# Chunked attention and a squared-ReLU feed-forward layer: one values step moved into an output stage, one transpose moved to the end of an input stage, and four steps moved by half a slot

## The chip, the cores and the metric

The kernel runs on one core of one Trainium2 chip. The metric is the device time of one execution in microseconds (us), as the median of several runs. The profile comes from one further execution of the same program. Its span, from the first to the last instruction, is a little shorter than the device time of that execution.

The engines are named as in the profile: PE is the matrix engine, PEld its weight loads (they overlap PE), DVE the vector engine, ACT the scalar engine, POOL the GpSimd engine, and SP the engine whose queue issues the loads and the transposes by DMA. Every engine works its instructions off in the order in which the program gives them.

## The reference, cut to what matters

```python
# q, k, v: [8, 8, 576, 64]; attention inside chunks of 64 tokens
scores = q_c @ k_c.T / 8
attn = exp(scores - max); attn = attn / (sum + 1e-9)
out = attn @ v_c
x = out.transpose(0, 2, 1, 3).reshape(4608, 512)
h = maximum(x @ w_in, 0)          # w_in  [512, 2048]
y = (h * h) @ w_out               # w_out [2048, 512]
```

Inputs and output are float32; the matrix products are done in bf16 with float32 sums.

## The kernel before, in words

The 4608 tokens are 18 groups of 256, numbered 0 to 17, and two groups make a block, 0 to 8. A block passes through three kinds of work.

*Attention of a group.* The loads of q, k and v are issued on SP. q and k are cast to bf16 (`C`) and transposed by DMA (`TD`). `scores` (`SC`, L474 and the exponential on ACT, L485) makes 32 small matmuls and one ACT instruction. `values` (`AV`, or its halves `AV0` and `AV1` for the group's first and second 128 tokens) makes 16 small matmuls of L501 a half into a bank of PSUM. DVE then takes the reciprocal of the sums (L435) and multiplies (L436), which gives x. `transpose_x` (`XT`) makes eight transposes on PE (L531) into a bank of PSUM and one copy on ACT (L536), which gives a half of xT. For blocks 6 and 8 it is a DMA instead.

*Input stage* of blocks 0 to 3: for each of 16 slices of 128 hidden units (`ft` 0 to 15), four matmuls of 512 columns (L570), a ReLU on ACT (L581), and the square on DVE (L588) or ACT (L586). The result is gT. For blocks 4 to 8 the stage goes in 16 "quads" of seven products (`A1`, `B2`, `A6`, `C5`, `A7`, `C3`, `A4`, L647, four matmuls of 256 columns each), a form of fast matrix multiplication with seven products in place of eight. DVE adds two partial results and takes the ReLU (L655), ACT copies partial results out (L683, L689, L692), and the square falls to ACT (L664), DVE or POOL (L666).

*Output stage*: block 0 goes plainly (L883). From block 1 on there are seven products of 16 matmuls each (L766) in the same fast form, over sums of gT that DVE makes (`g_sum`, L604: `d4`, `d5`, `d3`, `d2`). The first two products of block 2 are `p2`, which needs no sum, and `p1`, which needs `d4`. `d4` is made in two halves, the first at slot 14 of the input stage, the second at slot 15. After `p1` ACT copies its bank out (`keep`, L823), and the third product may add to that bank only when the copy has been made.

The order of everything is written out by hand. Blocks 0 to 3 have a plan by *slot*: one slot per `ft` (0 to 15), then one per half product of the output stage. For block 2, slots 16 to 18 are empty; 19 and 20 are `p2`, 21 and 22 are `p1`, and 23 to 32 the other five. After the work of a slot come one load and then what the plan has there, in the order in which it was entered: the sums, then `C`, `TD`, `SC`, `AV`, `XT`. From block 4 on there are four slots a quad step, and a block takes 16 slots. In slot s come first the products of the quads, then what the plan has at s − 0.5, then the half product of the block before (if the slot has one), then what the plan has at s. So 9.5 is the place in slot 10 ahead of that slot's output half, and 10 the place behind it.

While block 2 goes through its stages, the attention is that of block 3 (groups 6 and 7). While block 4 does, it is that of block 5 (groups 10 and 11); during block 6 it is that of block 7 (groups 14 and 15, whose chunks lie in different batch rows).

The PSUM banks of the attention: through block 3, `att_bank` gives `ps_att` and `ps_att2` by turns. From block 4 on there is one tile only, `ps_att`, so each user waits until the one before it has been read out:

```python
def att_bank():
    if "out" in banks:
        return ps_att.tile([128, 1024], FP32, name="ps_att")
    state["att"] = state.get("att", 0) + 1
    if state["att"] % 2:
        return ps_att.tile([128, 1024], FP32, name="ps_att")
    return ps_att2.tile([128, 1024], FP32, name="ps_att2")
```

Of the kernel before, what the change touches and what calls it, by code (L numbers as in the profile page):

```python
# [144 lines left out]
def kernel(  # L145
# [31 lines left out]
    def is_whole(g):  # L177
        return chunks[g][0][0] == chunks[g][3][0]
# [5 lines left out]
    QUADS = 4  # L184
# [130 lines left out]
    def go(pieces):  # L315
        for f in pieces:
            f()
# [288 lines left out]
    def summed(out, in0, in1, op=ALU.add):  # L606
        return lambda *_: add(out, in0, in1, op)
# [28 lines left out]
    def tock():  # L636
        state["clock"] += 1
        for x in [x for x in later if x[0] <= state["clock"]]:
            later.remove(x)
            x[1]()  # L640
# [268 lines left out]
    def pieces(grps):  # L909
        for g in grps:  # L910
            yield from qk_pieces(g)
        for g in grps:
            yield from v_pieces(g)

    SC, AV, XT = scores, values, transpose_x
    TD = transpose_qk_dma
# [67 lines left out]
    for j in range(QUADS):  # L984
        grps, nxt, far = blocks[j], blocks[j + 1], blocks[j + 2]
        plan = {}

        def at(slot, f, *x):
            plan.setdefault(slot, []).append((f, x))

        if j == 0:
            loads, go_slots = pieces(far), range(17)
            at(28, summed(b11_p_b21, b11, b21))
            for slot, f in ((24, TA), (27, SC), (29, AV), (31, XT)):
                at(slot, f, nxt[0])
            at(31, TQ, nxt[1])
            at(31, summed(b22_m_b21, b22, b21, ALU.subtract))
            phases = [first_ffn_in, ffn_out_by_ft(0)]
        elif j == 1:
            loads, go_slots = itertools.chain(*map(qk_pieces, far)), range(26, 48)  # L1000
            for slot, f in ((1, TK), (4, SC), (7, AV), (12, XT)):
                at(slot, f, grps[1])
            for i, g in enumerate(nxt):
                for slot, f in ((16 + 4 * i, C), (21 + 4 * i, TD), (36 + i, SC), (38 + 2 * i, AV),
                                (41 + 2 * i, XT)):
                    at(slot, f, g)
            for i, g in enumerate(far):
                at(36 + 4 * i, C, g)
                at(42 + 3 * i, TD, g)
            at(2, summed(b12_p_b21, b12, b21))  # L1010
            at(12, summed(b11_m_b12, b11, b12, ALU.subtract))
            at(20, summed(b12_p_b22, b12, b22))
            out_j = ffn_out(1)
            for i in (20, 27, 29, 31):
                at(i, lambda: next(out_j)())
            phases = [ffn_in(1, [(0, 256, FT_ORDER), (256, 256, FT_ORDER)]), out_j]
        else:
            out_j = ffn_out(j)
            for i in (14, 15):
                at(i, lambda: next(out_j)())  # L1020
            phases = [ffn_in(j, [(0, BT, range(n_ft))])]
            if j == 2:
                loads, go_slots = itertools.chain(*map(v_pieces, nxt), pieces(far)), [
                    *range(16), *range(27, 36)]
                slots = {SC: (6, 9), AV: (11, 14), XT: (22, 28), C: (21, 26), TD: (25, 29)}
                for f in (C, TD):
                    for i, g in enumerate(far):
                        at(slots[f][i], f, g)
                phases.append(out_j)
            else:  # L1030
                loads, go_slots = pieces(far), range(11)
                for f, slots in ((C, (11, 13)), (TD, (13, 15))):
                    for i, g in enumerate(far):
                        at(slots[i], f, g)
                slots = {SC: (2, 4), AV: (7, 10), XT: (13, 15)}
            for f in (SC, AV, XT):
                for i, g in enumerate(nxt):
                    at(slots[f][i], f, g)
            if j == 2:
                for i, f in enumerate((summed(a21_p_a22, a21, a22),  # L1040
                                       summed(a12_m_a21, a12, a21, ALU.subtract),
                                       summed(a11_p_a21, a11, a21))):
                    at(1 + 2 * i, f)
        slot = 0
        for phase in phases:
            for _ in phase:
                if slot in go_slots:
                    for f in loads:
                        f()
                        break  # L1050
                for f, x in plan.get(slot, []):
                    f(*x)
                slot += 1
        assert all(x < slot for x in plan), (j, slot, sorted(plan))
        if j < QUADS - 1:
            go(loads)
# [19 lines left out]
    for j in range(QUADS, n_blk):  # L1076
        if j == QUADS:
            n = 14 - LEAD
            slots = [1 + 19 * i // n for i in range(n)]
            assert len(slots) == n  # L1080
        else:
            slots = [s for s in range(4, 20) if s % 16 not in NO_OUT]
            start = 3
        if j == QUADS:
            between = {}
            for n in (0, 1, 2, 3):
                between.setdefault(n, []).append((load, (1, loads)))
            for n in (2, 2, 2, 3):
                between.setdefault(n, []).append((x_sums, (QUADS, len([1 for z in between.values() for y in z if y[0] is x_sums]))))
            for f, x in between.get(0, []):  # L1090
                f(*x)
            for i in range(LEAD):
                next(out_j)
                tock()
                for f, x in between.get(i + 1, []):
                    f(*x)
        else:
            outs[j - 1] = ffn_out(j - 1)
            at(j, start, lambda j=j: next(outs[j - 1])())
        for s in slots:  # L1100
            plan.setdefault(("out", 16 * (j - QUADS) + s), []).append(outs[j - 1])

        if j + 1 < n_blk:
            S0, V0, V1, X0 = ((1.5, 3.5), (4.5, 7.5), (6, 9.5), (8, 11.5)) if j == QUADS else (
                (0.5, 7), (2, 8), (3.5, 9.5), (3.5, 10)) if is_whole(blocks[j + 1][0]) else (
                (3.5, 9.5), (5, 10.5), (7, 12), (8.5, 13.5))
            for i, g in enumerate(blocks[j + 1]):
                at(j, S0[i], SC, g)
                at(j, V0[i], AV0, g)
                at(j, V1[i], AV1, g)  # L1110
                at(j, X0[i], XT, g)
            if j + 2 == n_blk:
                at(j, 22, check_sums)
                at(j, 25.5, count_bad)
            for i, s in enumerate((13.5, 15, 17.5, 18)):
                at(j, s, x_sums, j + 1, i)
        if j == QUADS:
            for s in range(4):
                at(j, 4 * s + 2, w_sums_in_place, s)
            assert next(loads, None) is None  # L1120
        if j + 2 < n_blk:
            more = pieces(blocks[j + 2])
            if j == n_blk - 3:

                for s, n in ((0, 1), (1, 1), (2, 1), (3, 1), (4, 1), (5, 1), (10, 2), (12.5, 3),
                             (14, 1), (14.5, 1), (15, 1), (15.5, 1)):
                    at(j, s, load, n, more)
            else:
                for s in range(0, 16):
                    at(j, s, load, 1 if is_whole(blocks[j + 2][0]) else 2, more)  # L1130
            for i in range(2):
                at(j, (9, 13)[i], C, blocks[j + 2][i])
                at(j, ((9.5, 13.5) if j == n_blk - 3 else (12, 13.5))[i], TD, blocks[j + 2][i])
# [66 lines left out]
```

## Time and profile before

| | us |
|---|---|
| median of 3 runs | 283.7 (282.65 to 283.81) |
| the profiled execution | 284.07, with a span of 282.3 |
| PE busy | 268.1 (95% of the span) |
| DVE busy | 201.1 (71%) |
| ACT busy | 167.9 (59%) |
| POOL busy | 91.9 (33%) |
| granted PE clock | 0.997 |

In a row of the timeline the first number is the start in us from the start of the span, the second the duration of the group in us, then the engine, the line of the code, the operation, what it writes and reads, the shape, and how many instructions the row holds. In brackets stands how long the engine was idle before it, and on whom it waited. Durations of instructions in a row overlap a little, since each begins before the end of the one before has been recorded. So the step from one start to the next is what the engine needs for it.

Block 2's input stage begins at 82.91, its output stage at 98.70; block 3's input stage begins at 112.91. Quad 0 of block 4 begins at 133.71.

### The profile page before, as it was taken

Reading aid. Unit: us, or ns where it says so; the run is one execution under the profiler, and the core shown is the slowest. Engines: PE = TensorE matmul, PEld = TensorE weight load, DVE = VectorE, ACT = ScalarE, POOL = GpSimd, SP = SyncE. Lnnn points to the kernel's source line nnn. Section 1 sums busy time; section 2 is a strip of 40 time slices with the busy share of each in tenths; the row PEclk is TensorE's granted clock in tenths of the full one; section 3 lists DMA queues with packets and bytes.
Section 4 is the critical chain, followed back from the end, with each engine's and each line's share of the span. In section 5 each row is a group of like instructions: output and inputs, shape, how many; then the busy total and the mean of one; then the engine's idle time right before and its main releaser. Section 6 shows DMA issues by size and latency. Waiting matters only on the chain.

```text
span 282.3 us, 8007 instructions
## 1 busy us (share of the span) xinstructions
PE 268.1 (95%) x3304; PEld 205.6 (73%) x3307; DVE 201.1 (71%) x367; ACT 167.9 (59%) x298; POOL 91.9 (33%) x123
## 2 busy tenths in 40 slices
PE   2989999999999989999989999999999999999994
PEld 2764444788774479447878888888788888888883
DVE  1287605899448591399989998789679877994751
ACT  1527705786448855875767775665766664756330
POOL 2047832430350002132233525442343322431612
PEclk9999999999999999999999999999999999999998
DMA  7999999999999995999999788599997340220323
GB/s 221 240 323 393 393 308 247 343 202 162 298 179 231 219 243 117 260 249 182 229 239 198 173 213 217 117 193 231 253 165 196 77 58 18 85 64 10 76 75 111
DMA packets 133368, 55.09 MB, mean 195 GB/s; under 512 B 102160, under 2 KB 129040, under 8 KB 133328
## 3 DMA queue, kind: packets, MB, share of 16 engines
q1 hardware_dynamic: 130320, 45.23, 69.7%
q0 software_dynamic: 2864, 9.18, 9.9%
q8 instruction: 27, 0.44, 0.6%
q10 hardware_dynamic: 144, 0.13, 0.1%
q14 instruction: 13, 0.11, 0.1%
HBM read 36.70 MB, written 9.44 MB: 163 GB/s over the span
## 4 chain that ended last, share of the span: by engine, by line
PE 81%; DVE 11%; ACT 3%; DMA 2%; issue 1%; SPq 0%; ACTq 0%; DVEq 0%
PE ps_ffn L647 21%; PE ps_out L766 20%; PE ps_ffn L570 15%; PE ps_ffn L766 13%; PE ps_ffn L883 5%; DVE x L436 3%; DVE gT L588 3%; PE ps_att L474 2%; PE ps_att L501 2%; DMA qk_st<-in_k_dram 2%; DVE w_st L604 2%; PE ps_att L531 1%; PE ps_ffn L426 1%; PE ps_ffn L393 1%; DVE relu L655 1%
## 5 line engine op out<-in xcount | busy, mean ns | idle before, releaser
L570 PE MATMUL ps_ffn<-xT,w_in_bf 128*128 128x512 bf16 (+1 forms) x328 | 58.7, 333 | 1.2 <-DVE xT L517 1.0
L766 PEld LDWEIGHTS <-w_st 128*128 128x128 bf16 x512 | 48.9, 98 | 8.0 <-DVE w_st L604 1.7
L655 DVE CUSTOM_DVE_ANT_0 relu<-ps_ffn,w_st 128x512 f32<-128x512 f32 x60 | 39.3, 684 | 15.2 <-PE ps_ffn L647 13.8
L581 ACT ACTIVATE relu<-ps_ffn 128x256 bf16<-128x256 f32 (+2 forms) x82 | 39.9, 503 | 12.7 <-PE ps_ffn L570 11.2
L570 PEld LDWEIGHTS <-w_in_bf 128*128 128x128 bf16 x328 | 30.9, 98 | 22.5 <-DVE xT L517 1.2
L588 DVE TENSOR_TENSOR gT<-relu 128x256 bf16<-128x256 bf16 (+2 forms) x69 | 34.3, 529 | 17.3 <-ACT relu L581 16.9
L795 POOL DMA_DIRECT2D out_dram<-o_sb x27 | 19.8, 732 | 52.1 <-DVE o_sb L604 50.1
L647 PE MATMUL ps_ffn<-qk_st,w_in_bf 128*128 128x256 bf16 x240 | 35.3, 273 | 0.0
L647 PEld LDWEIGHTS <-w_in_bf 128*128 128x128 bf16 x320 | 30.7, 98 | 4.0 <-issue 0.2
L766 PE MATMUL ps_out<-w_out_bf,w_st 128*128 128x256 bf16 x240 | 31.0, 273 | 0.4 <-DVE w_st L604 0.4
L766 PEld LDWEIGHTS <-gT 128*128 128x128 bf16 x296 | 28.5, 98 | 3.5
L689 ACT ACTIVATE w_st<-ps_ffn 128x512 f32<-128x512 f32 x20 | 11.9, 597 | 26.7 <-PE ps_ffn L647 26.7
L436 DVE TENSOR_TENSOR x<-ps_att,recs 128x512 bf16<-128x512 f32 x36 | 24.9, 691 | 1.2
L647 PEld LDWEIGHTS <-qk_st 128*128 128x128 bf16 x240 | 22.6, 98 | 2.9
L485 ACT ACTIVATE e<-ps_att 128x1024 bf16<-128x1024 f32 x18 | 18.4, 1024 | 9.5 <-PE ps_att L474 9.5
L647 PE MATMUL ps_ffn<-xT,qk_st 128*128 128x256 bf16 x160 | 23.9, 273 | 0.0
L666 POOL TENSOR_TENSOR qk_st<-relu 128x512 bf16<-128x512 f32 x10 | 10.3, 1033 | 41.6 <-DVE relu L655 38.1
L666 POOL TENSOR_TENSOR gT<-relu 128x512 bf16<-128x512 f32 x10 | 10.3, 1033 | 38.6 <-DVE relu L655 38.6
L766 PE MATMUL ps_ffn<-w_out_bf,w_st 128*128 128x256 bf16 x144 | 17.7, 273 | 0.5 <-DVE w_st L604 0.5
L664 ACT ACTIVATE gT<-relu 128x512 bf16<-128x512 f32 x28 | 17.7, 632 | 0.0
L604 DVE TENSOR_TENSOR w_st<-gT,w_st 128x1024 bf16<-128x1024 bf16 x26 | 17.5, 706 | 0.0
L445 POOL CAST qkb<-qk_st 128x1024 bf16<-128x1024 f32 x12 | 13.9, 1156 | 10.2 <-DMA qk_st<-in_k_dram 10.2
(91 smaller groups left out, 433.5 us busy)
## 6 DMA issues: line engine op xcount, KB each, us to landing
qk_st<-in_q_dram SPq DMA_DIRECT2D x16, 512.0 KB, 5.2
out_dram<-o_sb POOLq DMA_DIRECT2D x31, 256.0 KB, 4.1
qk_st<-in_k_dram SPq DMA_DIRECT2D x24, 256.0 KB, 5.4
ve_sb<-in_v_dram SPq DMA_DIRECT2D x32, 128.0 KB, 4.1
w_st<-in_moe_w_in_dram SPq DMA_DIRECT2D x8, 512.0 KB, 6.3
w_st<-in_moe_w_out_dram SPq DMA_DIRECT2D x8, 512.0 KB, 5.5
vo_sb<-in_v_dram SPq DMA_DIRECT2D x24, 128.0 KB, 3.4
qk_st<-in_k_dram SPq DMA_DIRECT2D x4, 512.0 KB, 6.0
```

What stands on the lines that cost most here:

```text
L436: nc.vector.tensor_tensor(out=x, in0=o[:, :, :, 0:D], in1=rec.to_broadcast([128, 2, n, D]), op=ALU.mult)
L485: nc.scalar.activation(out=e_out, in_=s_in, func=AF.Exp, scale=scale)
L570: nc.tensor.matmul(out=h[:, 0:n], lhsT=w_in_bf[:, dt, ft * 128:(ft + 1) * 128], rhs=xT[:, c // 128:(c + n) // 128, dt, :], start=(dt == 0) ...
L581: nc.scalar.activation(out=rl[:, 0:n], in_=h[:, 0:n], func=AF.Relu)
L588: nc.vector.tensor_tensor(out=dst, in0=src, in1=src, op=ALU.mult)
L604: nc.vector.tensor_tensor(out=out, in0=in0, in1=in1, op=op)
L647: nc.tensor.matmul(out=bank[:, f * GT:(f + 1) * GT], lhsT=a[:, dt, ft * 128:(ft + 1) * 128], rhs=b[:, :, dt, :], start=(first and f == 0 a ...
L655: nc.vector._custom_dve(TENSOR_ADD_SAT, out=out, in0=in0, in1=in1, s0=BIG, s1=0.0)
L664: engine.activation(out=dst, in_=r, func=AF.Square)
L666: engine.tensor_tensor(out=dst, in0=r, in1=r, op=ALU.mult)
L766: nc.tensor.matmul(out=out_ps, lhsT=lhsT, rhs=b[:, i, :], start=(first and i == 0 and (last or t == 0)), stop=(i == HF - 1), skip_group_ch ...
L795: dma.dma_start(out=out[t0:t0 + GT, col:col + HD].rearrange("(t p) d -> p t d", p=128), in_=o_sb.rearrange("p (t d) -> p t d", d=HD))
```

## The change

In the plan of block 2:

- `AV` of group 7 (both halves: 32 matmuls, two reciprocals, two multiplications) goes from slot 14, ahead of `ft` 15, to slot 22, behind `p1`.
- `XT` of group 6 (eight transposes, one copy on ACT) goes from slot 22 to slot 15, behind `ft` 15 and ahead of `p2`.

In the plan of block 4, for block 5's groups 10 and 11:

- `AV1` of group 11 goes from 9.5 to 10, behind the output half of slot 10.
- `XT` of group 10 goes from 8 to 8.5, behind the two products (`B2`, `C3`) of slot 9. Slot 9 has no output half.
- `XT` of group 11 goes from 11.5 to 12, behind the output half of slot 12.

In the plan of block 6, for block 7's group 15:

- `AV0` goes from 10.5 to 11, behind the output half of slot 11.

No instruction is added or removed; no tile and no load changes.

```diff
@@ j == 2 @@
-                slots = {SC: (6, 9), AV: (11, 14), XT: (22, 28), C: (21, 26), TD: (25, 29)}
+                slots = {SC: (6, 9), AV: (11, 22), XT: (15, 28), C: (21, 26), TD: (25, 29)}
@@ j >= QUADS @@
-            S0, V0, V1, X0 = ((1.5, 3.5), (4.5, 7.5), (6, 9.5), (8, 11.5)) if j == QUADS else (
+            S0, V0, V1, X0 = ((1.5, 3.5), (4.5, 7.5), (6, 10), (8.5, 12)) if j == QUADS else (
                 (0.5, 7), (2, 8), (3.5, 9.5), (3.5, 10)) if is_whole(blocks[j + 1][0]) else (
-                (3.5, 9.5), (5, 10.5), (7, 12), (8.5, 13.5))
+                (3.5, 9.5), (5, 11), (7, 12), (8.5, 13.5))
```

## The prediction

> **What bounds the kernel now.** I read the page's busy shares and the chain that ended last, then the waits of PE, then the timeline of each engine around the steps that move. PE carries the time, with 81% of the chain; by the page it is busy for 95% of the span, and its granted clock is 0.997.
>
> ```profile
> PE 81%; DVE 11%; ACT 3%; DMA 2%; issue 1%; SPq 0%; ACTq 0%; DVEq 0%
> ```
>
> So a moved step is worth what it changes in PE's gaps. The waits view names them (engine and line, on whom; us in total, times, longest). The three rows below hold the gaps that the change touches: on a sum of gT, on x, and on the exponential.
>
> ```profile
> PEld L531 <- DVE x L436: 2.1, 4, 1.0
> PEld L766 <- DVE w_st L604: 1.7, 3, 0.8
> PEld L501 <- ACT e L485: 1.1, 2, 0.7
> ```
>
> **A: block 2, values of group 7 to slot 22, first transpose to slot 15.** PE's rows now:
>
> ```profile
> 97.41 0.22 PE L501 MATMUL ps_att<-ve_sb,e 64*64 64x65 bf16 x2
> ...
> 97.82 1.04 PE L570 MATMUL ps_ffn<-xT,w_in_bf 128*128 128x512 bf16 x4
> 98.70 1.91 PE L766 MATMUL ps_ffn<-w_out_sum,gT 128*128 128x256 bf16 x16
> 100.44 0.60 PE L766 MATMUL ps_ffn<-w_out_bf,w_st 128*128 128x256 bf16 x4
> 101.58 1.48 PE L766 MATMUL ps_ffn<-w_out_bf,w_st 128*128 128x256 bf16 x12 [0.53 <-DVE w_st L604]
> 102.89 0.61 PE L531 MATMUL ps_att<-ident,x 128*128 128x128 bf16 x8
> 103.73 1.91 PE L766 MATMUL ps_ffn<-w_out_sum,w_st 128*128 128x256 bf16 x16 [0.23 <-ACT kept L823]
> ...
> 108.97 0.61 PE L531 MATMUL ps_att<-ident,x 128*128 128x128 bf16 x8
> 109.42 1.91 PE L766 MATMUL ps_ffn<-w_out_bf,gT 128*128 128x256 bf16 x16
> ```
>
> By starts, values take 0.41 (97.41 to 97.82), ft 15 0.88, p2 1.74 for 16 matmuls (0.109 each), p1 as much, eight transposes 0.45 (108.97 to 109.42). p1 stops after four matmuls, at 100.88, and goes on at 101.58: 0.70 of wait for d4's second half. DVE shows why:
>
> ```profile
> 98.69 0.20 DVE L435 RECIPROCAL recs<-ps_att 128x8 f32<-128x8 f32 x1
> ...
> 100.38 0.42 DVE L588 TENSOR_TENSOR gT<-relu 128x512 bf16<-128x512 bf16 x1
> 100.83 0.69 DVE L604 TENSOR_TENSOR w_st<-gT 128x1024 bf16<-128x1024 bf16 x1
> 101.43 2.49 DVE L604 TENSOR_TENSOR w_st<-gT,w_st 128x1024 bf16<-128x1024 bf16 x4
> ...
> 105.05 0.68 DVE L604 TENSOR_TENSOR o_sb<-ps_ffn,kept 128x512 f32<-128x512 f32 x1
> ```
>
> Group 7's two pairs of reciprocal and multiplication (98.69 to 100.38, 1.69) stand ahead of the square of ft 15, and that ahead of d4's second half. Without them the square waits only for its ReLU on ACT:
>
> ```profile
> 98.20 0.63 ACT L586 ACTIVATE gT<-relu 128x512 bf16<-128x512 bf16 x1
> 98.90 0.60 ACT L581 ACTIVATE relu<-ps_ffn 128x512 bf16<-128x512 f32 x1
> 99.39 1.04 ACT L442 CAST qkb<-qk_st 128x1024 bf16<-128x1024 f32 x1
> ...
> 103.09 0.59 ACT L823 COPY kept<-ps_ffn 128x512 f32<-128x512 f32 x1 [1.72 <-PE ps_ffn L766]
> 103.58 1.02 ACT L536 COPY xT<-ps_att 128x1024 bf16<-128x1024 bf16 x1
> ```
>
> The changed order, step by step. PE: ft 15 at 97.41 to 98.29, transposes to 98.74, p2 to 100.48, p1's first four to 100.92. ACT: the ReLU follows the square of 98.20 at 98.83, done 99.43. DVE: square 99.46, d4's second half 0.45 later (as 100.38 to 100.83), done about 100.6. That is 0.3 ahead of PE, so the 0.70 goes. p1 ends at 102.22. Then the values take their 0.41 where the transposes lay, in the shadow of ACT's copy of p1's bank. That copy comes 0.20 after the last matmul is issued (102.89 to 103.09) and frees the bank 0.64 later (103.73), so the third product starts at 102.22 + 0.84 = 103.06 against 103.73. **A gives 0.7.**
>
> What queues behind the moved pieces. On ACT, the transpose's copy (1.02) now runs ahead of group 8's casts: 99.32, 100.3, 101.3, free at 102.3, just before `keep` is due at 102.42. Even if each runs 0.1 long, PE loses 0.2. The casts end about 0.9 later, and with them TD of group 8 on SP and the three loads of v behind it; even the longest landing shown below, 7.7, has group 8's transposed q and k there by 110.1, ahead of block 3's stage (112.9). None of the moved steps issues a DMA, and none touches POOL. On DVE, group 7's 1.69 now stands behind the six remaining sums (2.49 for four, so 3.7) and the output sum (0.6): 100.6 + 3.7 + 0.6 + 1.7 = 106.6. Its transpose is due on PE at 108.97 − 0.7 = 108.3, so 1.7 to spare: no cost. The banks alternate as before, and each is read out in time (group 6's transpose copy by 100.3, the values need it at 102.2).
>
> **B: block 4, half steps.** There is one attention bank now.
>
> ```profile
> 144.92 1.05 PE L766 MATMUL ps_out<-w_out_sum,gT 128*128 128x256 bf16 x8
> 146.73 0.62 PE L531 MATMUL ps_att<-ident,x 128*128 128x128 bf16 x8 [0.77 <-DVE x L436]
> 147.19 0.60 PE L647 MATMUL ps_ffn<-xT,qk_st 128*128 128x256 bf16 x4
> ...
> 148.06 0.60 PE L647 MATMUL ps_ffn<-qk_st,qk_st 128*128 128x256 bf16 x4
> ```
> ```profile
> 145.99 0.69 DVE L436 TENSOR_TENSOR x<-ps_att,recs 128x512 bf16<-128x512 f32 x1
> 147.93 1.29 DVE L655 CUSTOM_DVE_ANT_0 relu<-ps_ffn,w_st 128x512 f32<-128x512 f32 x2 [1.25 <-PE ps_ffn L647]
> ```
>
> The output half ends at 144.92 + 0.87 = 145.79. Group 10's transpose wants the bank that group 11's first values hold until DVE has multiplied (146.68), and goes at 146.73: 0.94 idle. Moved behind B2 and C3 (147.19 to 148.06, 0.87), these fill 145.79 to 146.66; the transpose still goes at 146.73, and slot 10 follows at 147.18 in place of 148.06. **B gives 0.88**, if nothing is late next. B2 and C3 need banks, sums and weights that were all read or written by 145.8.
>
> Late next could be two steps, and the other two half steps bear on them. Group 11's second values need the bank when ACT has copied group 10's transpose, 147.35 + 1.02 = 148.4. At 9.5 they would come at 148.05 and wait 0.3; at 10 they come behind an output half, at 148.92. Group 11's transpose needs x from DVE: two ReLU sums from 146.7 to 148.0, the output sum when slot 10's half is done (149.1), a square of 0.6, then 0.83 for the pair, 151.2. At 12 it comes at 148.92 + 0.36 + 1.31 + 0.87 = 151.46 (values with their switch, three products, the half). So 0.25 to spare.
>
> **C: block 6, group 15's first values behind the output half of slot 11.**
>
> ```profile
> 200.59 0.60 PE L647 MATMUL ps_ffn<-qk_st,w_in_bf 128*128 128x256 bf16 x4
> 201.57 0.22 PE L501 MATMUL ps_att<-ve_sb,e 64*64 64x65 bf16 x2 [0.38 <-ACT e L485]
> ...
> 201.83 1.05 PE L766 MATMUL ps_out<-w_out_bf,w_st 128*128 128x256 bf16 x8
> 202.71 0.60 PE L647 MATMUL ps_ffn<-qk_st,w_in_bf 128*128 128x256 bf16 x4
> ```
>
> The product ends at 201.03 and the values wait for the exponential until 201.57. With the half first (0.87, its sum d3 written by 200.1) they go at 202.0, the exponential long done, and slot 12 follows at 202.26 against 202.71. **C gives 0.45.** Group 15's multiplication comes 0.4 later, done 203.4; the second values want the bank at 204.1.
>
> **Sum.** 0.70 + 0.88 + 0.45 = 2.03. Against the profiled execution 284.07 − 2.03 = 282.0; it was 0.37 above the median, so 283.7 − 2.03 = **281.7**. Half a per cent, 1.4 us, is about what a measurement of this kernel can tell from no change.
>
> **The rivals.** *First, POOL's casts fall on other DVE work in block 3.* DVE sets PE's wait there, and the casts are timed by loads.
>
> ```profile
> 128.95 1.51 POOL L445 CAST qkb<-qk_st 128x1024 bf16<-128x1024 f32 x1 [1.48 <-DMA qk_st<-in_k_dram]
> ```
> ```profile
> 129.48 1.52 DVE L604 TENSOR_TENSOR w_st<-gT 128x1024 bf16<-128x1024 bf16 x1
> ...
> 131.64 0.69 DVE L604 TENSOR_TENSOR w_st<-gT 128x1024 bf16<-128x1024 bf16 x1
> ```
> ```profile
> 132.39 1.48 PE L766 MATMUL ps_out<-w_out_bf,w_st 128*128 128x256 bf16 x12 [0.43 <-DVE w_st L604]
> ```
>
> The same sum takes 1.52 beside the cast and 0.69 without. If loads, casts and DVE all move 0.7 earlier, nothing changes. If the casts stay where the loads put them, one can newly fall on a square in the chain: +0.83, 282.5. Or the sum at 129.48 gets ahead of its cast: DVE gains 0.83, of which PE can use only its wait at this place, 0.4 as the row has it and 0.6 by the starts: 281.1. The Trainium skill ("SBUF — State Buffer", Who interferes with whom) says that a VectorE instruction with two SBUF inputs and a GpSimd instruction that reads SBUF share a read port, and that the later one is blocked until the first ends. By that rule, 1.52 against 0.69 agrees, and the order of issue, not my sum, would decide between 281.1 and 282.5.
>
> *Second, the wait of B comes back.* Its slack is 0.25 on DVE for group 11's x. If DVE runs behind there, PE stops at the second transpose in place of the first, and the 0.88 is lost: 282.6. Against it: DVE stood idle 1.25 ahead of 147.93, and that room is used in the new order.
>
> *Third, slower: the DMA stream does not follow.* From 112 on the loads run close behind one another on SP.
>
> ```profile
> DMA to landing us min/median/max: 4.4/5.2/7.7
> ```
> ```profile
> 129.53 4.38 SPq L451 DMA_TRANSPOSE qkT<-qkb  x2
> ```
> ```profile
> 135.98 0.44 PE L474 MATMUL ps_att<-qkT 64*64 64x64 bf16 x32
> ```
>
> Group 10's q and k are transposed by a DMA issued at 129.53; at the median landing they are there at 134.7, and their scores, after A at 135.3, have 0.6 to spare even if SP does not move. At the longest landing, 7.7, they are there at 137.2 and PE waits 1.9. Two such landings, in this block and the next, would cost 3.8: 281.7 + 3.8 = 285.5. It decides from a landing of about 5.8 on; the change is lost altogether where two land at 6.8. Against it: SP waits in block 2 for the casts of group 9 on ACT, which follow PE, so its stream moves with PE.
>
> **Chances.** Forecast 0.60 (own range 281.2 to 282.2); casts on other DVE work 0.14; B's wait back 0.11; DMA late 0.13; something else 0.02. Range: 280.9 (the 281.1 of the first rival less some spread) to 283.3 (both middle rivals together, 281.7 + 0.83 + 0.88 = 283.4, nearly), which leaves out the DMA case. Faster by over 0.5% (below 282.3): 0.64, the forecast and the good side of the first rival. Within: 0.22, the middle rivals. Slower: 0.14.
>
> **What would show it.** In A: no wait of PE on w_st between p1's fourth and fifth matmul, values between p1 and the third product, this about 5.65 after the end of ft 14 (now 6.32). In B: no gap ahead of L531 in slot 9, and quad products before it. In C: no wait on the exponential at L501. Wrong it would be by a new wait of PE on ACT's `keep` in block 2, on x at group 11's transpose, or on qkT at L474, or by a longer run of DVE in block 3.

## The result and the profile after

The changed kernel takes 281.47 us (median of 6 runs, 280.87 to 282.20) against 283.22 (6 runs, 282.65 to 283.81) of the kernel before, measured beside it: a ratio of 0.9937, with a 95% interval of 0.9916 to 0.9959. Medians are of all runs and ratios of the fast ones (slow is a run over 1.5% above its kernel's fastest), so a ratio need not be that of the two medians. The forecast was 281.7. The profiled execution took 282.2, with a span of 280.4, and the granted clock is 0.999.

First the shares of the chain that ended last, on the page after:

```profile
PE 77%; DVE 8%; DMA 6%; SPq 4%; ACT 2%; issue 1%; POOL 0%; ACTq 0%; DVEq 0%
```

PE has 77% of it, where it had 81%, and DMA with SP's queue 10%, where they had 2%; 8.3 us (2.9% of the span) of this are one landing, that of group 9's transposed q and k, to which block 3 below comes back. PE's work is the same (267.8 of busy time on the page, 268.1 before), so what was gained was gained in its gaps. The waits view has them (engine and line, on whom; us in total, times, longest):

```profile
PEld L766 <- DVE w_st L604: 1.2, 2, 1.0
...
PEld L501 <- ACT e L485: 0.4, 1, 0.4
...
PEld L531 <- DVE x L436: 0.4, 2, 0.2
```

Against the three rows of before, the transposes' wait on x fell from 2.1 to 0.4, the values' wait on the exponential from 1.1 to 0.4, and the output products' wait on w_st from 1.7 to 1.2, with a longest that rose from 0.8 to 1.0: one of those gaps is gone and another one grew.

**A in the timeline.** PE, around the end of block 2's input stage and its first output products:

```profile
97.47 0.61 PE L531 MATMUL ps_att<-ident,x 128*128 128x128 bf16 x8
97.92 1.91 PE L766 MATMUL ps_ffn<-w_out_sum,gT 128*128 128x256 bf16 x16
99.66 1.91 PE L766 MATMUL ps_ffn<-w_out_bf,w_st 128*128 128x256 bf16 x16
101.50 0.22 PE L501 MATMUL ps_att<-ve_sb,e 64*64 64x65 bf16 x2
...
102.25 1.91 PE L766 MATMUL ps_ffn<-w_out_sum,w_st 128*128 128x256 bf16 x16 [0.28 <-DVE w_st L604]
```

The transposes, p2 and p1 follow one another without a stop, all 16 matmuls of p1 stand in one row, and the third product follows p2 after 4.33 (97.92 to 102.25), where it was 5.03 (98.70 to 103.73). DVE and ACT at the same place:

```profile
98.64 0.43 DVE L588 TENSOR_TENSOR gT<-relu 128x512 bf16<-128x512 bf16 x1 [0.57 <-ACT relu L581]
99.10 0.69 DVE L604 TENSOR_TENSOR w_st<-gT 128x1024 bf16<-128x1024 bf16 x1
```
```profile
98.51 1.00 ACT L536 COPY xT<-ps_att 128x1024 bf16<-128x1024 bf16 x1
...
100.62 1.04 ACT L445 CAST qkb<-qk_st 128x1024 bf16<-128x1024 f32 x1 [0.16 <-DMA qk_st<-in_k_dram]
101.61 0.59 ACT L823 COPY kept<-ps_ffn 128x512 f32<-128x512 f32 x1
```

The square no longer stands behind group 7's multiplications, and d4's second half is done at 99.8, ahead of the fifth matmul of p1 (99.66 + 0.44). ACT gets the transposes' copy and both casts out of the way just as `keep` is due; `keep` ends at 102.20 and the third product starts at 102.25, so it is `keep`, and not the sum that the row names, that it waits for.

**B.** PE in slots 8 to 12 of block 4 and at the first product of block 5:

```profile
144.12 1.05 PE L766 MATMUL ps_out<-w_out_sum,gT 128*128 128x256 bf16 x8
145.01 0.60 PE L647 MATMUL ps_ffn<-xT,qk_st 128*128 128x256 bf16 x4
145.45 0.60 PE L647 MATMUL ps_ffn<-xT,w_in_bf 128*128 128x256 bf16 x4
145.94 0.62 PE L531 MATMUL ps_att<-ident,x 128*128 128x128 bf16 x8
146.39 0.60 PE L647 MATMUL ps_ffn<-qk_st,qk_st 128*128 128x256 bf16 x4
...
150.69 0.61 PE L531 MATMUL ps_att<-ident,x 128*128 128x128 bf16 x8
...
153.75 1.30 PE L647 MATMUL ps_ffn<-qk_st,w_in_bf 128*128 128x256 bf16 x8
154.89 0.60 PE L647 MATMUL ps_ffn<-xT,qk_st 128*128 128x256 bf16 x4
```

B2 and C3 (145.01 and 145.45) fill what was the gap, and the transposes wait for nothing. From the output half to the first product of slot 10 it was 3.14 (144.92 to 148.06) and is 2.27 (144.12 to 146.39). The last two rows hold what was not foreseen: eight matmuls (two products) take 1.14 to the next start, where they took 0.88 before. These are the rows of before:

```profile
155.42 1.04 PE L647 MATMUL ps_ffn<-qk_st,w_in_bf 128*128 128x256 bf16 x8
156.30 0.60 PE L647 MATMUL ps_ffn<-xT,qk_st 128*128 128x256 bf16 x4
```

The second of the two products in the row of eight is block 5's first, A1, and it reads a sum of xT that DVE makes. DVE and POOL after:

```profile
149.78 0.69 DVE L436 TENSOR_TENSOR x<-ps_att,recs 128x512 bf16<-128x512 f32 x1
...
151.32 1.88 DVE L655 CUSTOM_DVE_ANT_0 relu<-ps_ffn,w_st 128x512 f32<-128x512 f32 x3
153.12 1.27 DVE L604 TENSOR_TENSOR qk_st<-xT 128x512 bf16<-128x512 bf16 x1
```
```profile
152.09 1.04 POOL L666 TENSOR_TENSOR gT<-relu 128x512 bf16<-128x512 f32 x1 [3.96 <-DVE relu L655]
153.07 1.04 POOL L442 CAST qkb<-qk_st 128x1024 bf16<-128x1024 f32 x1
```

And before:

```profile
152.52 0.68 DVE L655 CUSTOM_DVE_ANT_0 relu<-ps_ffn,w_st 128x512 f32<-128x512 f32 x1
...
154.75 0.83 DVE L604 TENSOR_TENSOR qk_st<-xT 128x512 bf16<-128x512 bf16 x1
```
```profile
154.27 1.04 POOL L442 CAST qkb<-qk_st 128x1024 bf16<-128x1024 f32 x1
```

In both, the sum starts while POOL casts and ends 0.27 to 0.28 after the cast (155.58 against 155.31 before, 154.39 against 154.11 after): by these rows it is the cast that times it. The cast follows POOL's square, and the square follows the first of DVE's three ReLU sums. That one came only 1.20 earlier (152.52 to 151.32): DVE's unbroken run of work ahead of it begins at 148.34, where it began at 149.41. The three now run in one go (1.88). A1 itself came 1.67 earlier: due at 155.42 + 0.44 = 155.86 before, with 0.28 to spare, and at 153.75 + 0.44 = 154.19 after, when the sum is 0.20 away. A1 starts at 154.45, 0.26 late.

**C.** PE in slot 11 of block 6:

```profile
199.18 0.60 PE L647 MATMUL ps_ffn<-qk_st,w_in_bf 128*128 128x256 bf16 x4
199.61 1.04 PE L766 MATMUL ps_out<-w_out_bf,w_st 128*128 128x256 bf16 x8
...
200.84 0.61 PE L647 MATMUL ps_ffn<-qk_st,w_in_bf 128*128 128x256 bf16 x4
```

From the product to slot 12 it is 1.66 (199.18 to 200.84), where it was 2.12 (200.59 to 202.71).

**Block 3**, where the change does nothing itself. PE, DVE and POOL after:

```profile
116.76 0.45 PE L474 MATMUL ps_att<-qkT 64*64 64x64 bf16 x32 [0.37 <-DMA qkT<-qkb]
...
131.59 1.48 PE L766 MATMUL ps_out<-w_out_bf,w_st 128*128 128x256 bf16 x12 [0.70 <-DVE w_st L604]
```
```profile
126.03 2.73 DVE L588 TENSOR_TENSOR gT<-relu 128x512 bf16<-128x512 f32 x3
128.69 1.52 DVE L604 TENSOR_TENSOR w_st<-gT 128x1024 bf16<-128x1024 bf16 x1
```
```profile
126.30 1.32 POOL L442 CAST qkb<-qk_st 128x1024 bf16<-128x1024 f32 x1 [0.96 <-DMA qk_st<-in_q_dram]
```

Before, DVE's row of three squares and POOL's cast were these:

```profile
127.68 1.88 DVE L588 TENSOR_TENSOR gT<-relu 128x512 bf16<-128x512 f32 x3
```
```profile
126.43 1.04 POOL L442 CAST qkb<-qk_st 128x1024 bf16<-128x1024 f32 x1 [0.89 <-DMA qk_st<-in_q_dram]
```

The cast starts at the same time as before (126.30 and 126.43, each time on the landing of its load), while the squares start 1.65 earlier and now meet it: 2.73 in place of 1.88. The wait at p1's fifth matmul grew from 0.43 to 0.70, and group 9's scores waited 0.37 for the transposed q and k. That DMA was issued earlier than before (108.45, before 109.92), as much earlier as PE came, but it took 8.3 to land, where it had taken 6.1.

By stages, from the weight load that opens each (us). The untouched start of the kernel, up to block 2, takes 81.5 to 83.0 in one execution or another, and the stages left out agree within 0.02 among these six. Four slots are one quad step; a block from 4 on has 16 slots and so four quads, not the 16 of the description above:

| stage | before | after | A alone | B alone | C alone | after, again |
|---|---|---|---|---|---|---|
| start to block 2 | 82.80 | 82.09 | 81.98 | 82.95 | 82.83 | 82.83 |
| block 2 | 30.00 | 29.22 | 30.83 | 30.00 | 30.00 | 29.23 |
| block 3 | 20.80 | 21.49 | 21.41 | 21.10 | 20.80 | 20.81 |
| block 4, slots 8 to 11 | 6.92 | 6.04 | 6.91 | 6.04 | 6.92 | 6.04 |
| block 4, slots 12 to 15 | 5.25 | 5.61 | 5.25 | 5.61 | 5.25 | 5.61 |
| block 5, slots 0 to 3 | 5.65 | 5.55 | 5.65 | 5.56 | 5.65 | 5.55 |
| block 6, slots 8 to 11 | 8.20 | 7.84 | 8.20 | 8.20 | 7.84 | 7.84 |
| block 6, slots 12 to 15 | 7.36 | 7.27 | 7.36 | 7.36 | 7.27 | 7.27 |
| span | 282.30 | 280.43 | 282.90 | 282.14 | 281.87 | 280.52 |

A weight load usually opens about 0.1 ahead of its matmul, and a load that had to wait does not. So the wait of 0.26 at A1 shows as 0.36 in slots 12 to 15, and the next stage gives 0.10 of it back; the two rows belong together.

In the first profile of the changed kernel 0.71 of the span's 1.87 comes from a start that the change doesn't touch, and about as much is lost again in block 3 (0.69: some 0.45 at group 9's scores, counted by their weight loads, and 0.27 at p1). Whether that loss belongs to the change is what the first experiments had to settle.

### The profile page after: what moved, and what is told of

Its sections match the earlier page's. It is cut to its first block, busy times and chain, and to the rows that moved or that the text cites. A ratio compares the mean times of both kernels' runs of the same rounds, so it can differ in the third digit from the quotient of the medians.

```text
span 280.4 us, 8006 instructions
## 1 busy us (share of the span) xinstructions
PE 267.8 (95%) x3307; PEld 205.2 (73%) x3307; DVE 200.3 (71%) x367; ACT 168.2 (60%) x298; POOL 91.8 (33%) x123
## 4 chain that ended last, share of the span: by engine, by line
PE 77%; DVE 8%; DMA 6%; SPq 4%; ACT 2%; issue 1%; POOL 0%; ACTq 0%; DVEq 0%
PE ps_ffn L647 21%; PE ps_out L766 21%; PE ps_ffn L570 14%; PE ps_ffn L766 11%; PE ps_ffn L883 5%; DMA qkT<-qkb 3%; DMA w_st<-in_moe_w_in_dram 3%; PE ps_att L501 2%; DVE gT L588 2%; PE ps_att L474 2%; DVE w_st L604 2%; SPq L266 1%; PE ps_att L531 1%; SPq L307 1%; DVE x L436 1%
## 5 line engine op out<-in xcount | busy, mean ns | idle before, releaser
L588 DVE TENSOR_TENSOR gT<-relu 128x256 bf16<-128x256 bf16 (+2 forms) x69 | 32.5, 500 | 20.4 <-ACT relu L581 20.1
L442 POOL CAST qkb<-qk_st 128x1024 bf16<-128x1024 f32 x12 | 12.8, 1065 | 15.6 <-DMA qk_st<-in_q_dram 15.6
```

The source lines that it names most:

```text
L588: nc.vector.tensor_tensor(out=dst, in0=src, in1=src, op=ALU.mult)
```

## The experiments

The theory: PE's gaps are the price, the three parts are independent, and each is worth what its stage shows. The rivals are those of the prediction: a gain that DVE's meeting with POOL eats up in block 3, a wait that comes back in block 4, and a DMA stream that doesn't follow.

**Each part alone.** Of the change, A alone keeps the plan of block 2, B alone the line of block 4, C alone that of block 6:

```diff
# A alone
-                slots = {SC: (6, 9), AV: (11, 14), XT: (22, 28), C: (21, 26), TD: (25, 29)}
+                slots = {SC: (6, 9), AV: (11, 22), XT: (15, 28), C: (21, 26), TD: (25, 29)}
# B alone
-            S0, V0, V1, X0 = ((1.5, 3.5), (4.5, 7.5), (6, 9.5), (8, 11.5)) if j == QUADS else (
+            S0, V0, V1, X0 = ((1.5, 3.5), (4.5, 7.5), (6, 10), (8.5, 12)) if j == QUADS else (
# C alone
-                (3.5, 9.5), (5, 10.5), (7, 12), (8.5, 13.5))
+                (3.5, 9.5), (5, 11), (7, 12), (8.5, 13.5))
```

> Only the moves in block 2 (values of group 7 to slot 22, transpose of group 6 to slot 15). Theory 1, every microsecond of PE's gap counts to the end: 0.7 us faster than before, ratio 0.9975; block 2's stages (from its first input matmul to block 3's) 0.75 shorter, block 3's input stage as long as before, 20.8. Theory 2, the gain is given back in block 3, where PE then waits for the DMA that transposes group 9's q and k, or DVE's sums come late: block 2 shorter by the same 0.75, but block 3 (from its first input matmul to quad 0 of block 4) longer by 0.4 to 0.8, ratio 0.999 to 1.0.

> Only the three half steps of block 4. Theory 1: 0.88 us faster, ratio 0.997, no gap ahead of group 10's transpose, and block 5 begins 0.88 earlier after quad 0 of block 4. Theory 2, part of it is given back where DVE's first sum for block 5 runs beside POOL's casts: about 0.6 us faster, ratio 0.998, with 0.2 to 0.3 of wait at the first product of block 5.

> Only group 15's first values behind the output half of slot 11 in block 6. Both theories: 0.45 us faster, ratio 0.9984, which is at the limit of what the rounds can tell; in the trace, no wait on the exponential at the small matmuls of slot 11, and slot 12 begins 0.45 earlier after slot 11's product.

Measured against 283.15 before: A alone 282.91, ratio 0.9990 (0.9972 to 1.0007); B alone 282.48, 0.9986 (0.9967 to 1.0005); C alone 282.92, 0.9993 (0.9977 to 1.0009). None can be told from 1 by its times. The stages say more. C is −0.36 and −0.09 and nothing else: 0.45. B is −0.88, then +0.36 in the next stage and −0.09 in the one after: 0.61, the same figures as in the whole change, so the late sum belongs to B and not to the execution. Block 2 of A alone shows 30.83, as its values of group 6 waited 1.41 for a load of v that comes ahead of any moved step:

```profile
PE ps_att L501 <- DMA vo_sb<-in_v_dram: 1.4, 1, 1.4
```

30.83 − 1.41 = 29.42, 0.58 under before; what follows such a stop need not run as it did, so the next run has the better figure for A. Its block 3 is 0.61 longer, about as in the first profile of the changed kernel, but here all of it stands at p1 (waits of 0.13 and 0.72 on w_st) and none on the transposed q and k. The profiled executions of A alone and B alone were the slowest of their runs, so what waited in them need not wait in the median one.

**The changed kernel again**, no edit.

> The changed kernel once more, all three parts, beside the kernel before. If the gains simply reach the end (theory 1): 2.0 us faster, ratio 0.993. If A is given back in block 3 and a part of B in block 5 (theory 2), the parts that stay are 0.0 to 0.3 of A, 0.62 of B and 0.45 of C: 1.1 to 1.4 us faster, ratio 0.995 to 0.996. In the trace block 3 (first input matmul to quad 0 of block 4) takes 21.1 to 21.5 rather than 20.8 where its third cast on POOL falls on DVE's squares.

281.66 against 283.42, ratio 0.9929 (0.9901 to 0.9957). Here block 2 gains 0.77 and block 3 gives nothing back (20.81). PE's wait in block 3, and DVE and POOL beside it:

```profile
131.65 1.48 PE L766 MATMUL ps_out<-w_out_bf,w_st 128*128 128x256 bf16 x12 [0.44 <-DVE w_st L604]
```
```profile
126.33 0.69 DVE L436 TENSOR_TENSOR x<-ps_att,recs 128x512 bf16<-128x512 f32 x1
126.94 1.88 DVE L588 TENSOR_TENSOR gT<-relu 128x512 bf16<-128x512 f32 x3
128.74 0.69 DVE L604 TENSOR_TENSOR w_st<-gT 128x1024 bf16<-128x1024 bf16 x1
```
```profile
125.83 1.04 POOL L442 CAST qkb<-qk_st 128x1024 bf16<-128x1024 f32 x1 [1.03 <-DMA qk_st<-in_q_dram]
...
128.88 1.44 POOL L445 CAST qkb<-qk_st 128x1024 bf16<-128x1024 f32 x1 [2.01 <-DMA qk_st<-in_k_dram]
```

The casts fall otherwise: the one at 125.83 lies over the multiplication at 126.33, which takes its usual 0.69, and is over at 126.87, before the three squares; the one at 128.88 comes behind the sum, which then takes 0.69. So the same program has 0.44 of wait at one time and 0.70 at another. That the place of the casts makes the difference is read from the rows; no run moved the casts alone. Among the profiles whose squares in block 3 are as before, the block is 0.6 to 0.7 longer than 20.80 in two of the six that have A, and 0.3 longer in one of the four that have no part of it. Here the span is accounted for to 0.03: 0.77 + (0.88 − 0.36 + 0.10) + 0.45 = 1.84, less 0.03 at the start, against 282.30 − 280.52 = 1.78.

Block 2 is not always so short. Of the nine profiles with A, four have 29.22 to 29.24. The other five have 29.41 to 30.83, three of them by waits for DMA ahead of every moved step (1.41 in A alone, 0.34 in two kernels below). The four without any part of A have 30.00 each. No run shows why these waits stood beside A and not there.

**One half step of B.** Only the transpose of group 10 is moved; group 11's second values and transpose stay:

```diff
-            S0, V0, V1, X0 = ((1.5, 3.5), (4.5, 7.5), (6, 9.5), (8, 11.5)) if j == QUADS else (
+            S0, V0, V1, X0 = ((1.5, 3.5), (4.5, 7.5), (6, 9.5), (8.5, 11.5)) if j == QUADS else (
```

> Of the half steps of block 4 only the first: group 10's transpose from 8 to 8.5, while group 11's second values stay at 9.5 and its transpose at 11.5. If the first step makes the gain and the other two protect it: PE waits 0.3 at group 11's second values for the bank that ACT is copying out, and at most 0.3 more at group 11's transpose for x, so 0.3 to 0.6 us faster, ratio 0.998 to 0.999. If the other two are not needed: 0.88 faster as with all three, ratio 0.997.

282.79 against 283.15, ratio 0.9999 (0.9979 to 1.0019). Slots 8 to 11 take 6.33, so the gain there is 0.59 of the 0.88, and PE's row of the values shows where the rest is:

```profile
148.32 0.22 PE L501 MATMUL ps_att<-ve_sb,e 64*64 64x65 bf16 x2 [0.23 <-ACT xT L536]
```

That is the wait of 0.3 for ACT's copy that the prediction gave to values left at 9.5. Slots 12 to 15 stay at 5.25: with this half step alone A1's sum is not late. So the first half step alone has 0.59, and all three together 0.62 (0.88 less 0.36, and 0.10 back): the other two win 0.29 in slots 8 to 11 and lose nearly all of it at A1's sum. No wait stands at group 11's transpose left at 11.5. The times can't tell this kernel from the one before; the profiled execution was the slowest of the twelve, and in it group 12's scores waited 1.72 on the transposed q and k in block 5.

**The values moved, the transpose left.** From the kernel before, in block 2:

```diff
-                slots = {SC: (6, 9), AV: (11, 14), XT: (22, 28), C: (21, 26), TD: (25, 29)}
+                slots = {SC: (6, 9), AV: (11, 22), XT: (22, 28), C: (21, 26), TD: (25, 29)}
```

> The kernel before, with only the values of group 7 moved to slot 22, and the transpose of group 6 left there, behind them. If A's gain comes from DVE's order alone and the transpose is moved for tidiness: the wait on d4 goes, both pieces lie in the shadow of ACT's copy of p1's bank, and block 2 is 0.8 to 1.1 shorter. If the banks decide: the two banks go by turns, so the transpose now takes the bank of the first half of the values, and PE waits until DVE has multiplied it, behind the six sums: until 105 to 105.6 by the starts of the profile before, so the third product starts near 106 in place of 103.73, block 2 is about 2.2 longer, ratio 1.007.

287.34 against 283.85, ratio 1.0171 (1.0095 to 1.0246). Block 2 takes 32.82, 2.82 more than before. PE and DVE there:

```profile
104.98 0.62 PE L531 MATMUL ps_att<-ident,x 128*128 128x128 bf16 x8 [3.17 <-DVE x L436]
```
```profile
104.23 0.69 DVE L436 TENSOR_TENSOR x<-ps_att,recs 128x512 bf16<-128x512 f32 x1
```

The two banks go by turns. With the values ahead of the transposes and both in the same stage, the transposes take the bank that the first values filled, and that is read out only when DVE has been through the sums and come to the multiplication: 3.17. So the moved transpose is no second gain beside the moved values but what makes them possible. The expectation had 2.2; of the 2.82, 0.29 is a DMA wait at 93.86. Outside block 2, group 12's scores waited 1.35 on a DMA in block 5.

**A1's sum earlier.** In the changed kernel the first sum of block 5's xT, which DVE makes during block 4, goes from slot 13.5 to slot 12, ahead of the last ReLU sums:

```diff
-            for i, s in enumerate((13.5, 15, 17.5, 18)):
+            for i, s in enumerate((12 if j == QUADS else 13.5, 15, 17.5, 18)):
```

> The changed kernel, with DVE's first sum for block 5 at slot 12 of block 4 in place of 13.5, ahead of the ReLU sums of slot 13 and of POOL's casts of group 13. If the 0.27 that block 5's first product loses in the changed kernel comes from that sum being late: no wait there, the stretch from the quad step of slot 12 to that of slot 16 back from 5.61 to 5.25 to 5.35, and 0.27 less in all, ratio 0.001 below that of the changed kernel. If it comes from something else (the transpose behind the output half, say), the stretch stays at 5.61.

282.50 against 283.42, ratio 0.9949 (0.9917 to 0.9980). Slots 12 to 15 are back at 5.25, and the sum takes 0.42 clear of POOL:

```profile
152.33 0.42 DVE L604 TENSOR_TENSOR qk_st<-xT 128x512 bf16<-128x512 bf16 x1
```

So it was that sum. The kernel gained nothing that the times show: in its profile PE then stood 0.78 at group 12's scores, again on the transposed q and k, and 0.34 at group 7's in block 2.

```profile
158.16 0.45 PE L474 MATMUL ps_att<-qkT 64*64 64x64 bf16 x32 [0.78 <-DMA qkT<-qkb]
```

**Squares of block 3 to ACT.** In the changed kernel, the square of ft 12, and in a second kernel squares of ft 10, 12 and 3 in place of the usual ones:

```diff
# ft 12 too
-            if (n == 512 and ft in SQUARES_ON_ACT) or (n < 512 and ft in (12, 3)):
+            if (n == 512 and (ft in SQUARES_ON_ACT or (j == 3 and ft == 12))) or (n < 512 and ft in (12, 3)):
# 3, 10 and 12
-            if (n == 512 and ft in SQUARES_ON_ACT) or (n < 512 and ft in (12, 3)):
+            if (n == 512 and ft in ((10, 12, 3) if j == 3 else SQUARES_ON_ACT)) or (n < 512 and ft in (12, 3)):
```

> The changed kernel, with one square of block 3 (ft 12) on ACT in place of DVE, which takes 0.6 off DVE's work ahead of d4. If DVE's run of squares and sums, lengthened by POOL's casts, sets the wait at p1 in block 3: that wait goes from 0.7 to 0.1 or 0.2, block 3 takes 20.2 to 20.8, and the kernel is 0.5 faster than the changed one. If ACT becomes the bound: PE waits for ReLUs on ACT in ft 13 to 15, no gain or a loss of up to 0.5.

> The changed kernel, with block 3's squares on ACT those of ft 3, 10 and 12 in place of 3, 10 and 14. ACT's work stays the same, but the one ahead of the last ReLU goes earlier. If DVE's end before d4 depends on that last ReLU as well as on its own squares: the wait at p1 in block 3 goes from 0.45 (0.7 with a third cast on it) to 0.1 or less, block 3 takes 20.3 to 20.5, 0.3 to 0.5 faster than the changed kernel. If DVE's run of squares alone sets it: no change, since it has as many squares as before.

The first: 281.74 against 283.42, ratio 0.9933 (0.9903 to 0.9964), block 3 20.64. The second: 282.98 against 283.56, 0.9963 (0.9927 to 1.0000), block 3 21.40. In the first the wait falls to 0.30, and now it is ACT that is behind: DVE's square waits 1.02 for the ReLU.

```profile
129.49 0.82 DVE L588 TENSOR_TENSOR gT<-relu 128x512 bf16<-128x512 f32 x1 [1.02 <-ACT relu L581]
```

The second has two waits, 0.18 and 0.72, at p1; there DVE's sum stands behind a cast (128.83) and takes 1.52, and two squares wait 0.36 and 0.32 for ReLUs on ACT. So one square less on DVE takes 0.14 off p1's wait (0.44 to 0.30) and 0.17 off the block, too little for the times to show, and ACT is then late itself. The second kernel does not decide between its two readings, since a cast fell on the sum.

**Group 9's scores later, and group 12's transposes earlier**, each in the changed kernel:

```diff
# scores of group 9
-                slots = {SC: (2, 4), AV: (7, 10), XT: (13, 15)}
+                slots = {SC: (2, 6), AV: (7, 10), XT: (13, 15)}
# transposes of group 12
-                at(j, ((9.5, 13.5) if j == n_blk - 3 else (12, 13.5))[i], TD, blocks[j + 2][i])
+                at(j, ((9.5, 13.5) if j == n_blk - 3 else (10.5 if j == QUADS else 12, 13.5))[i], TD, blocks[j + 2][i])
```

> The changed kernel, with group 9's scores in block 3 two slots later (6 in place of 4; the values stay at 10), which gives the DMA that transposes its q and k 1.7 us more. If that DMA is what sometimes holds PE there: no wait for it in the trace, and up to 0.4 faster than the changed kernel where it held, 0 where it did not, so 0 to 0.3 in the median. If the scores' exponential then comes late for ACT and the values: a wait of PE at group 9's values in slot 10, slower by 0.2 to 0.5.

> The changed kernel, with the transposing DMA of group 12 entered at slot 10.5 of block 4 in place of 12, so that it stands ahead of two loads of v in SP's queue (its cast is done by 148.2, and it is issued at about 151). If it is SP's queue that takes group 12's slack away as PE moves forward: issued by 149.5 after a start of quad 0 at 132.9, no wait of PE on qkT at group 12's scores in any profile, and a time equal to the changed kernel's in executions without that wait and 0.8 to 1.7 lower in those with it; median 0 to 0.3 lower. If the loads that it now holds up are needed first: a wait of PE at group 12's or 13's values in block 5, slower.

The first took 283.27 against 283.42, ratio 0.9987 (0.9955 to 1.0020): no gain, and 1.6 above the changed kernel measured at the same time. Its profile (block 3 20.81, no wait on qkT) doesn't show why; the second profile of the changed kernel had no such wait either. The second has six times between 281.07 and 287.78, too far apart to say anything. In its profile (span 280.34) the DMA does what was expected: issued at 149.01, group 12's q and k land 3.1 ahead of their scores, where it was 1.3 in the first profile of the changed kernel. But a wait of 0.30 on qkT stands at group 14's scores in block 6 (187.00). In block 2 `keep` came late there, since the cast ahead of it on ACT waited 0.36 for its load, and PE waited 0.42 for `keep` in place of 0.28. Whether the waits on DMA can be avoided is not shown.

**All three together**: A1's sum at slot 12, group 12's transposes at 10.5, and block 3's squares 3, 10 and 12 on ACT, in the changed kernel.

> The changed kernel with three further moves: block 5's first sum at slot 12, the transposing DMA of group 12 at 10.5, and block 3's squares on ACT those of ft 3, 10 and 12. If the three places are what is left of the waits behind the change: 0.3 less in block 4, 0.3 to 0.5 less in block 3, no wait on qkT, so 0.6 to 0.8 below the changed kernel, ratio 0.990 to 0.991 against the kernel before. If waits only change their place: the ratio of the changed kernel, 0.993.

282.09 against 283.56, ratio 0.9960 (0.9924 to 0.9996), with a span of 280.05. That is not better than the changed kernel, and 0.6 to 0.8 was expected. A1's wait is gone (5.25, with 5.65 in the next stage as in the kernel before, so 0.26 in all), but 0.19 comes back in block 5's second stage (6.80 against 6.61), where the small matmuls at 160.39 wait for DVE's multiplication, and block 3 is at 21.44. Block 6's second stage is 0.29 longer too (7.27 against 6.98): there group 14's scores wait on the transposed q and k (186.71). So the expectation "no wait on qkT" did not hold either.

## Why the prediction was right

The forecast of 281.7 stands against 281.47 (and 281.66 when it was measured again). Its mechanism is that of the trace, but not every term is. That the time agrees so closely is in part luck: it was worked out from a median of 283.7 over three runs, which came to 283.22 over six, and the gain was 1.75 where 2.03 had been forecast. In the sum an A that was too small stands beside a B that was too large.

*A, 0.70.* Block 2 gained 0.78 and 0.77 where nothing else held it up. The 0.08 more is the step into the small matmuls: ft 14 ended at about 97.31 before (sixteen matmuls of the kind take 3.47 after, 94.00 to 97.47, and its twelve began at 94.71), the values began at 97.41, and the prediction started ft 15 at 97.41. Each other step of the working is there: the ReLU bounds the square, d4's second half is in time, the values lie in the shadow of `keep`, which ACT reaches just in time after the copy and two casts. "The banks alternate as before" was right, and the kernel with the values moved alone shows what hung on it (3.17). What the working left out is that the casts ahead of `keep` wait for loads: where one lands late, `keep` comes late too (0.14 more wait in the kernel with group 12's transposes moved).

*B, 0.88.* The gap went in full (6.92 to 6.04), and the half step alone gave 0.59 there, as expected. The two protecting half steps were tried only together. They win 0.29 in these slots, but with them A1's sum is late, so in all they are worth 0.03. The slack of 0.25 at group 11's transpose came out at 0.2 (x written at 150.47, the transposes at 150.69), so the second rival did not happen. **The step that failed is "if nothing is late next".** The working looked at the next two users of the attention's bank and at x, but not at the next *sum* that DVE owes to PE. A1's sum had 0.28 to spare, and it stands behind a cast on POOL that moved up by 1.20 where PE moved up by 1.67. B is worth 0.62, not 0.88. It is the first rival's mechanism in a block where the prediction did not look for it. That the sum at its old place is the cause is shown by the early sum, which takes the 0.36 (0.26 with the next stage) away. That the cast makes it late is read from the rows (at the 0.42 that it takes alone it would have been written at 153.54, in time) and was not tried by itself.

*C, 0.45.* Measured 0.45 (0.36 and 0.09), in every kernel that has it.

*Sum, 2.03.* By stages it is 1.84, and by the medians 1.75 and 1.76. The first rival is real but undecided by the program: the same kernel has 0.70 or 0.44 of wait in block 3, by where the casts fall. The gain is there, and 0.3 to 0.7 of it is lost in some executions: nearer the runs don't come. The Trainium skill ("SBUF — State Buffer", Who interferes with whom) has it that a VectorE instruction with two SBUF inputs contends with a GpSimd one that reads SBUF, and that the order of issue decides which of them is blocked. By that rule the rows agree on the order: the sum took 1.27 where the cast was issued 0.05 ahead (153.07 and 153.12), and 0.69 where the sum came 0.14 ahead of its cast (128.74 and 128.88), the cast then taking 1.44. They are a little short of a whole block: a sum of 0.42 that ran only after the cast would end 0.42 behind it, and it ends 0.27 to 0.28 behind.

The third rival, the slower one, showed in single profiles as waits on qkT of up to 1.72. The longest landing in the profile before, 7.7, was no bound: the changed kernel has 8.3 at group 9, and that is its wait of 0.37. So two of the signs that the prediction had named against itself did show in the first profile, a wait on qkT and a longer run of DVE in block 3; the second profile has neither. Neither profile of the changed kernel has two such waits, and its medians don't carry the rival.

What stays open. The medians of A, B and C alone are 0.24, 0.67 and 0.23 under before, 1.14 in all, where the whole change gives 1.75; each interval is about 0.5 us to either side, and wider for the whole, so this is no proof that the parts help one another, and nothing in the stages says that they do. How often A gives something back in block 3 would take more profiles than there are. No run isolated what makes a landing long.

## What to carry to other kernels

When a gap of the bound engine is filled, go on past it until *every* result that another engine owes it has been checked against the new due time, the sums for the next stage too, and not only the users of the bank that had caused the gap. A step moved among banks that go by turns moves the turn: find the step that must move with it before pricing the first. Work that loads set off need not move when PE does, so an earlier stage can meet it at other places; where the meeting costs, price a gain with and without it.

## What the runs showed that had not been expected

Beside a cast on POOL, DVE's instructions fall into two kinds. The page after has the mean of those that read PSUM and at most one SBUF operand (busy us, mean ns, then idle before):

```profile
L655 DVE CUSTOM_DVE_ANT_0 relu<-ps_ffn,w_st 128x512 f32<-128x512 f32 x60 | 39.3, 685 | 12.6 <-PE ps_ffn L647 11.4
...
L436 DVE TENSOR_TENSOR x<-ps_att,recs 128x512 bf16<-128x512 f32 x36 | 24.9, 692 | 1.2
```

The means of 60 and of 36 are 0.69 and so the duration of one alone, though POOL works beside many of them, as beside the one at 126.33 above; the squares and sums with both inputs in SBUF take 0.69 alone (0.42 the short sum of xT), and more when they come behind the start of a cast: 0.83 and 1.27 the short sum, 1.52 the sum of gT. So what was free on DVE is not the same everywhere: by these rows a multiplication under a cast costs nothing, and a sum there up to 0.85.

And SP's queue follows PE only in part. The transposes of group 12's q and k were issued here, after and before:

```profile
151.47 2.89 SPq L451 DMA_TRANSPOSE qkT<-qkb  x1
```
```profile
151.32 2.97 SPq L451 DMA_TRANSPOSE qkT<-qkb  x1
```

PE had moved up by 1.67 (A1's pair of products from 155.42 to 153.75), and SP's issue not at all. In the second profile of the changed kernel, which starts within 0.03 of the one before, the issue came 0.39 earlier (150.93) and group 12's scores 1.33 (158.57 to 157.24), while group 9's issue came 0.74 earlier (109.18), as much as PE. So the time that group 12's landing has until its scores need it shrank from 2.6 to 1.3 and 1.4.

Six of the fourteen profiles have such a wait on qkT behind block 1, of 0.22 to 1.72. Of the changed kernel, which alone has two profiles, one has 0.37 and the other none. Where group 12's scores waited, its landing took long: 6.4 in the kernel with the early sum (issued at 151.74, about as in the rows above), 6.3 in that with one half step (issued at 153.29) and 6.0 in that with the values moved alone (155.70). In the other eleven profiles it took 4.4 to 4.9. What makes a landing long was not shown.
